# Rows of the recurrence asked for five blocks ahead in every block, and scatters one by one behind GpSimd's diagonals

## The chip, the cores and the metric

The kernel runs on one core of a Trainium2 chip. Five engines work beside each other, each with its own instruction stream in order: TensorE (PE; its weight loads are listed as PEld), VectorE (DVE), ScalarE (ACT), GpSimd (POOL) and SyncE (SP), which issues nearly all plain DMAs. GpSimd issues the indirect DMAs, the scatters. The metric is the device time of one execution in microseconds.

## The reference

Two stages. A recurrence (batch 4, 8 heads, 768 steps, head size 48) gives rows of 8 x 48 = 384 numbers, one per token; a mixture of 8 experts sends each of the 3072 rows through the one expert with the largest logit.

```
state = 0                                   # per batch and head, 48 x 48
for t in range(768):
    cur    = (u * k_t) outer v_t
    y_t    = r_t @ (state + cur)
    state  = w_t[:, None] * state + k_t outer v_t      # w between 0.8 and 0.95

x = y as (3072, 384)
e   = argmax(x @ w_gate);  g = softmax(x @ w_gate)[e]
out = g * (relu(x @ w1[e]) @ w2[e])         # w1[e]: 384 x 1024, w2[e]: 1024 x 384
```

## The kernel before, in words

**Blocks.** The 768 steps are cut into 6 chunks of 128, times 4 batches: 24 blocks, chunk by chunk (block n is chunk n // 4, batch n % 4). Within a block the recurrence is products of 128 x 128 matrices: k times suffix products of w (`kh`) against r times prefix products of w (`rh`) gives the part inside the chunk (`ap`), which is merged through a causal mask into `at`, whose diagonal carries u; `at` times v plus the state's part (`yp`, from `gbd`) gives y.

**Order.** All engines run in the order in which `iteration(n)` writes the instructions; nothing is reordered. Iteration n, from -3 to 23, is a software pipeline: it prepares block n + 3 on VectorE (suffix scan, line 409; product, 421; prefix scan, 427; product, 369) and GpSimd (product rk, 362), turns block n + 1 (diagonals of `at` on ScalarE, 403, and GpSimd, 391) and finishes block n on TensorE and VectorE (`pe_a`, 531; merge by `copy_predicated`, 434; `pe_av`, 566). GpSimd's product of line 362 is held back until VectorE has finished the reciprocal behind the suffix scan (413), and its diagonal (391) until VectorE has finished the prefix scan of block n + 3 (427); both are marked as dependencies.

**Rows of blocks.** `load(n)` brings w, r and k of block n, 580.5 KB, into a ring of 6 buffers (line 111); `load_v(n)` brings v, 192 KB, into one of 5 (line 120). All plain DMAs go through SP's queue in order. The ring's buffer for block n + 6 is free once block n has been prepared, that is in iteration n - 3. Heads that don't fit the 128 partitions take a way through DRAM: `hop_out(n)` (two DMAs, 374) writes parts of `kh` and `rh`, and `hop_in(n)` (380) reads them back as `xk`; SP waits in front of the read for the landing of the write. `pe_a(n)` uses `xk` for its last heads; in block 0, 8 warming products (`pe_warm`, line 526) stand in front of those.

**When rows are asked for.** Blocks 0 and 1 come in parts before the loop, and the w part of block 2. Iterations -3 to 0 ask for block n + 5 (in -3 that is block 2, whole, and the k and r parts of block 2 are asked for again at the end of that iteration). Iteration 0 asks for blocks 6 and 7 as well, and from 1 on it is block n + 7:

```
        if n > 0:
            load(n + 7)
        ...
            load_v(n + 4)
        hop_in(n + 2)
        if n <= 0:
            load(n + 5)
        ...
        hop_out(n + 3)
```

**Routing.** When y of a whole chunk is there, logits, argmax and a running count give each token a row number in its expert's list in DRAM (`xs`). `scatter(c, bs)` (line 730) sends the 128 rows of each batch in `bs` there by an indirect DMA, followed by a small memset on GpSimd (736). `prefill(e)` (352) writes default rows into the part of an expert's list that may stay empty. Chunks 0 and 1 are scattered in iterations 10 to 15, chunks 2 and 3 in 18 to 21, chunk 4 in 23; most stand between GpSimd's product (362) and its diagonal (391).

**Experts.** The first expert's weights come in 12 parts from iteration `W0` on (`load_part`), and six of them are split into a high and a low half from `H0` on (ScalarE makes the high half, line 263). Behind iteration 21, `Part(0, 96)` reads the first 192 rows of expert 0's list (line 283), waiting for all scatters up to there; their transposes (317) stand at the end of iteration 22. Then the last chunk's rows are routed, the experts are sorted by count, and experts run one by one (lines 327, 339, 1019).

Of the kernel before, what the change touches and what calls it, by code (L numbers as in the profile page):

```python
# [17 lines left out]
B, H, S, D = 4, 8, 768, 48  # L18
E, DM, FF = 8, 384, 1024
# [27 lines left out]
PD = 2  # L47
XC = DM + 2
OOB = 1 << 20
W0, H0 = 9, 14  # L50
WMIN, WMAX = 0.7, 1.05


# [5 lines left out]
def rwkv_moe_kernel(ctx, tc, rkw, vv, ub, wgp, wg, w1, w2, wc, out):  # L59
# [36 lines left out]
    def xtile(shape, name):  # L96
        pool, tag = xbanks[nth["x"] % len(xbanks)]
        nth["x"] += 1
        return pool.tile(shape, F32, name=name, tag=tag)
# [3 lines left out]
    def load(n, parts=((0, RW),)):  # L103
        if n >= NB:
            return
        if n == 0:
            for i in range(LD):
                ring.append(ld.tile([P, 4 * XC], F32, name="rkwt", tag="rkwt"))
        t = ring[n % LD][:, 0:RW]
        for lo, hi in parts:  # L110
            nc.sync.dma_start(t[:, lo:hi], rkw[n][:, lo:hi])
        blk[n] = dict(
            w=t[:, 0:NW], r=t[:, NW:NW + NR].rearrange("p (q c) -> p q c", c=C),
            k=t[:, NW + NR:].rearrange("p (q c) -> p q c", c=KW))

    def load_v(n):
        if n >= NB:
            return
        v = ld.tile([P, DM], F32, name="vt", tag="vt", bufs=5)
        nc.sync.dma_start(v, vv[n])  # L120
        blk[n]["v"] = v
# [14 lines left out]
    def keep_warm(t, n):  # L136

        for i in range(n):
            nc.tensor.matmul(t, ones, wz[:, 0:t.shape[1]], start=True, stop=True)
# [210 lines left out]
    def prefill(e):  # L350
        rows = (CMAX - LEAST) // 4
        nc.sync.dma_start(xs[e, LEAST:CMAX, :].rearrange("(p j) c -> p j c", j=4), zrow[:rows].unsqueeze(1).broadcast_to([rows, 4, XC]))

    def real(n):
        return 0 <= n < NB
# [21 lines left out]
    def hop_in(n):  # L377
        if real(n) and "kr" in blk.get(n, ()):
            blk[n]["xk"] = t = xk[n % 3]
            nc.sync.dma_start(t, hop[n % 3])  # L380

    def head_rows(n, q, j):
        d = blk[n]
        rs = slice(64 * j, 64 * j + D)
        if q < NQ:
            return d["kh"][rs, q, 1:KW], d["rh"][rs, q, :]
        return d["xk"][rs, 1:KW], d["xk"][rs, KW:]
# [114 lines left out]
    def pe_warm(k):  # L502
        if k:
            keep_warm(xtile([P, BANK], "wrm")[:, 0:384], k)
# [15 lines left out]
    def pe_a(n):  # L520
        if real(n):
            d = blk[n]
            d["ap"] = psT.tile([P, 2, BANK], F32, name="ap", tag="t").rearrange("p j (q c) -> p j q c", c=C)
            for q in range(NP_):
                if n == 0 and q == NQ:
                    pe_warm(8)
                for j in range(2):
                    kh, rh = head_rows(n, q, j)
                    for i in range(2):
                        hs = slice(64 * i, 64 * i + 64)  # L530
                        nc.tensor.matmul(d["ap"][hs, j, q, :], kh[:, hs], rh, start=True, stop=True)  # L531
# [195 lines left out]
    def scatter(c, bs=range(B)):  # L727
        xr = ch["xr", c]
        for b in bs:
            i = nc.gpsimd.indirect_dma_start(out=xsf, out_offset=bass.IndirectOffsetOnAxis(ap=ch["pi", c, b], axis=0),  # L730
                                             in_=xr[:, b, :], in_offset=None, bounds_check=E * NTOK - 1, oob_is_err=False)
            for k in scat:
                tc.declare_no_dep(i.ins, k, reason="rows of different tokens")
            scat.append(i.ins)

            nc.gpsimd.memset(none, 0.0)
# [37 lines left out]
    def late_splits(half, ks):  # L774
        for k in ks:
            t, i, n, p = late[k]
            split_piece(t, stg[0, i], i, n, p, half)

    def iteration(n):
# [8 lines left out]
        lot = (ROUTED, 0, B)  # L788
        pair = (NCH - 1, 0, 2)
        if n > 0:  # L790
            load(n + 7)
        if 1 <= n <= E:
            prefill(n - 1)
        if W0 <= n < W0 + 12:
            i, p = divmod(n - W0, 3)
            if p == 0:
                stg[0, i] = wst.tile([P, 1536], F32, name="wst", tag="wst")
            load_part(stg[0, i], one, i, p)
        if n > 0:
            load_v(n + 4)  # L800
        hop_in(n + 2)
        if n <= 0:
            load(n + 5)
        if n == 0:
            load_v(2)
# [2 lines left out]
        act_g(n, (NQ,))  # L808
        act_y(n - 1)
        pe_a(n)  # L810
        if n == 0:
            dve_at(n)
# [16 lines left out]
            weigh(whole)  # L829
        if n == NB - 2:  # L830
            late_splits("h", range(0, 3))
        if n in (10, 11):
            scatter(0, (2 * n - 20, 2 * n - 19))
        if 12 <= n < 16:
            scatter(1, (n - 12,))
        if 18 <= n < 22:
            scatter(2 + (n - 18) // 2, (n % 2 * 2, n % 2 * 2 + 1)[0:1 if n == 18 else 2])
        if n == NB - 1:
            scatter(ROUTED)
        if whole and b == 1:  # L840
# [51 lines left out]
            load(2, PARTS[1:])  # L892
        if -3 < n < 0:
            load_v(n + 2)
        if n == 0:
            for i in (6, 7):
                load(i)
                load_v(i - 3)
        if n >= 0:
            pool_diag(n + 1)  # L900
        if n == 18:
            scatter(2, (1,))
        if n == NB - 1:
            scatter(c, (0, 1))
        if whole and b == 0:
# [429 lines left out]
```

## Time and profile before

| | us |
|---|---|
| median of 3 runs | 415.96 |
| the runs | 417.9, 415.96, 411.45 |
| the profiled execution's own time | 417.89 |
| its span, first to last instruction | 416.2 |
| TensorE busy | 389.2 (94%) |
| VectorE busy | 259.5 (62%) |
| ScalarE busy | 222.6 (53%) |
| GpSimd busy | 112.9 (27%) |

The mean granted clock of TensorE is 0.948 of its full speed of 2.4 GHz. The DMA engines moved 72.38 MB. Busy shares are means over stages: up to about 160 us the blocks run, with VectorE near full, and behind it the experts, with TensorE at 94% or more. So a stage is read from its own stretch: from the waits in it and from the order of the instructions, with their start and duration.

### The profile page before, as it was taken

To read this page: it belongs to the slowest core of one execution; us is meant where nothing else is said; L and a number is where in the kernel's file an instruction comes from. 1 tells how busy PE (TensorE), PEld (TensorE's weight loads), DVE (VectorE), ACT (ScalarE), POOL (GpSimd) and SP (SyncE) were. 2 spreads that over 40 slices of the span, in tenths; PEclk is the share of its full clock that TensorE was granted. 3 is DMA by queue.
4 is the path that set the end of the run, shared out by engine and by line. 5 is a ranking of instruction groups with operands and counts; after the bars stand their busy time and mean duration, and the time that the engine had idled before them with its cause. 6 is when DMAs were issued, how large, how long until landed. Compare 5 with 4: busy or idle time off the path is not lost.

```text
span 416.2 us, 10076 instructions
## 1 busy us (share of the span) xinstructions
PE 389.2 (94%) x3810; PEld 356.1 (86%) x3810; DVE 259.5 (62%) x522; ACT 222.6 (53%) x597; POOL 112.9 (27%) x174
## 2 busy tenths in 40 slices
PE   8775999989898979999898999999999999999994
PEld 6564988878787758989887899999999999999994
DVE  7585789998799453447758475374483582842321
ACT  3454698969797841316737374383473573630210
POOL 4152122674359343100110032032051060021002
PEclk9988699999999995599999999999999999999998
DMA  6589879899957421295959825825727617011001
GB/s 184 159 250 341 257 212 252 245 325 286 308 132 215 120 78 58 62 324 168 238 163 285 283 83 131 292 83 164 263 94 222 246 41 226 2 53 37 17 4 53
DMA packets 40785, 72.38 MB, mean 174 GB/s; under 512 B 6319, under 2 KB 28570, under 8 KB 40732
## 3 DMA queue, kind: packets, MB, share of 16 engines
q1 hardware_dynamic: 36124, 62.21, 48.7%
q0 software_dynamic: 4608, 9.48, 6.9%
q8 instruction: 31, 0.51, 0.5%
q14 instruction: 22, 0.18, 0.1%
HBM read 57.40 MB, written 14.61 MB: 173 GB/s over the span
## 4 chain that ended last, share of the span: by engine, by line
PE 63%; DVE 11%; DMA 11%; ACT 7%; issue 5%; SPq 2%; POOL 0%; another core or an unknown queue 0%; POOLq 0%; ACTq 0%; DVEq 0%
PE bank L327 24%; PE bank L1019 17%; PE opt L339 8%; DMA rkwt<-in_rkw_dram 4%; ACT at L403 2%; DVE suf L409 2%; DVE pre L427 2%; PE yq L573 2%; PE yp L566 2%; PE yp L544 2%; PE pt L317 2%; DMA xk<-hop 2%; PE ap L531 2%; PE op L1008 2%; DMA wct<-in_wc_dram 1%
## 5 line engine op out<-in xcount | busy, mean ns | idle before, releaser
L289 POOL DMA_INDIRECT out_dram<-ot,xg x26 | 35.9, 1382 | 164.7 <-DVE ot L1009 101.3
L327 PE MATMUL bank<-xl,w1h 128*128 128x384 f32 (+5 forms) x168 | 59.0, 352 | 0.0
L327 PE MATMUL bank<-xh,w1l 128*128 128x384 f32 (+5 forms) x168 | 58.7, 350 | 0.0
L265 DVE TENSOR_TENSOR w2l<-wst,w2h 128x512 fp32r<-128x512 f32 x48 | 30.8, 686 | 41.4 <-ACT w2h L263 41.2
L327 PE MATMUL bank<-xh,w1h 128*128 128x384 f32 (+5 forms) x168 | 52.7, 351 | 1.6 <-DVE hl L330 1.6
L403 ACT ACTIVATE at<-ident,ct 128x128 f32<-128x128 f32 x144 | 46.8, 392 | 0.1
L434 DVE COPY_PREDICATED at<-cmask,ap 128x1024 f32<-128x1024 int32 x24 | 31.4, 1309 | 20.8 <-PE ap L531 12.0
L730 POOL DMA_INDIRECT xs<-xr,pi x24 | 27.4, 1142 | 25.0 <-DVE xr L641 10.0
L327 PEld LDWEIGHTS bank<-xh,w1h 128*128 128x128 f32 x168 | 31.3, 188 | 2.8 <-DVE hl L330 2.0
L1019 PE MATMUL bank<-hhl,w2h 128*128 128x432 f32 (+4 forms) x120 | 33.5, 356 | 0.0
L362 POOL TENSOR_TENSOR rk<-rkwt 128x384 f32<-128x384 f32 x24 | 22.1, 919 | 40.0 <-DVE pre L413 29.3
L1024 ACT ACTIVATE oT<-bank 128x464 f32<-128x464 f32 (+4 forms) x15 | 7.8, 523 | 46.1 <-PE bank L1019 46.1
L265 DVE TENSOR_TENSOR w1l<-wst,w1h 128x512 fp32r<-128x512 f32 x48 | 31.2, 686 | 2.0 <-ACT w1h L263 2.0
L329 ACT ACTIVATE hhl<-bank 128x384 fp32r<-128x384 f32 (+7 forms) x35 | 16.4, 480 | 29.9 <-PE bank L327 20.9
L327 PEld LDWEIGHTS bank<-xh,w1l 128*128 128x128 f32 x168 | 31.6, 188 | 0.8
L327 PEld LDWEIGHTS bank<-xl,w1h 128*128 128x128 f32 x168 | 31.6, 188 | 0.7
L330 DVE SCALAR_TENSOR_TENSOR hl<-bank,hh 128x384 fp32r<-128x384 f32 (+7 forms) x37 | 19.3, 532 | 19.5 <-ACT hh L329 19.2
L263 ACT ACTIVATE w1h<-wst 128x512 fp32r<-128x512 f32 x48 | 28.8, 628 | 3.2 <-DMA wst<-in_w_dram 2.3
L566 PE MATMUL yp<-at,vt 128*48 128x128 f32 x384 | 29.6, 293 | 0.4 <-issue 0.4
L329 ACT ACTIVATE hh<-bank 128x384 fp32r<-128x384 f32 (+7 forms) x37 | 17.1, 473 | 21.5 <-PE bank L327 19.4
L263 ACT ACTIVATE w2h<-wst 128x512 fp32r<-128x512 f32 x48 | 27.4, 622 | 2.0 <-DMA wst<-in_w_dram 0.9
L330 DVE SCALAR_TENSOR_TENSOR hhl<-bank,hhl 128x384 fp32r<-128x384 f32 (+7 forms) x35 | 18.6, 541 | 13.7 <-ACT hhl L329 11.8
(172 smaller groups left out, 934.7 us busy)
## 6 DMA issues: line engine op xcount, KB each, us to landing
rkwt<-in_rkw_dram SPq DMA_DIRECT2D x22, 580.5 KB
wst<-in_w_dram SPq DMA_DIRECT2D x48, 256.0 KB
wst<-in_w_dram SPq DMA_DIRECT2D x14, 768.0 KB
vt<-in_vv_dram SPq DMA_DIRECT2D x24, 192.0 KB
wct<-in_wc_dram SPq DMA_DIRECT2D x24, 192.0 KB
xg<-xs SPq DMA_DIRECT2D x6, 579.0 KB
xk<-hop SPq DMA_DIRECT2D x24, 112.4 KB
xs<-zrow SPq DMA_DIRECT2D x8, 289.5 KB
```

Source lines behind the costliest of these rows:

```text
L263: nc.scalar.activation(hi, st[:, cs], AF.Copy)
L265: nc.vector.tensor_tensor(out=lo, in0=st[:, cs], in1=hi.bitcast(F32), op=ALU.subtract)
L289: i = nc.gpsimd.indirect_dma_start(out=out[:, :], out_offset=bass.IndirectOffsetOnAxis(ap=t.bitcast(I32)[:, q, DM + 1:DM + 2], axis=0), in ...
L327: nc.tensor.matmul(hp, a, x[:, j, :], start=(i == 0), stop=(i == 8))
L329: nc.scalar.activation(hh, hp, AF.Relu)
L330: nc.vector.scalar_tensor_tensor(out=hl, in0=hp, scalar=0.0, in1=hh.bitcast(F32), op0=ALU.max, op1=ALU.subtract)
L339: nc.tensor.matmul(op, hs[f][x == "l"][:, cs], w2v(wt, "h" if part == "hl" else "l", f), start=(i == 0), stop=(i == 23))
L403: nc.scalar.activation(blk[n]["at"][:, j, q], ident, AF.Copy, scale=blk[n]["ct"][:, head(q, j):head(q, j) + 1])
L434: nc.vector.copy_predicated(out=d["at"].rearrange("p j q c -> p (j q) c"), mask=cmask.unsqueeze(1).broadcast_to([P, 2 * NP_, C]), data=d[" ...
L566: nc.tensor.matmul(d["yp"][o:o + D, q % 2, q // 2, :], d["v"][:, h * D:(h + 1) * D], d["at"][:, j, q, :], start=(n < B and q < 2), stop=(q ...
L730: i = nc.gpsimd.indirect_dma_start(out=xsf, out_offset=bass.IndirectOffsetOnAxis(ap=ch["pi", c, b], axis=0), in_=xr[:, b, :], in_offset=No ...
L1019: nc.tensor.matmul(pp, w, a, start=(i == 0), stop=(i == 23))
```

## The change

The rows of block n + 5 are asked for in every iteration from -2 on; iteration -3 no longer asks for the whole block 2, and iteration 0 asks for nothing beyond block 5. v comes two blocks ahead in every iteration. The prefills start in iteration 2 instead of 1, the first expert's weight parts in 10 instead of 9, and their splits in 15 instead of 14. In block 0 three warming products stand in front of the last heads, not eight. The scatters of chunks 0 and 1 stand one per iteration in iterations 10 to 17, behind GpSimd's diagonal (`pool_diag`); of chunks 2 and 3 those of iterations 18 to 21 stand one behind the diagonal, and one or two at the old place from 19 on.

```diff
-W0, H0 = 9, 14
+W0, H0 = 10, 15
@@ pe_a
                 if n == 0 and q == NQ:
-                    pe_warm(8)
+                    pe_warm(3)
@@ iteration
         if n > 0:
-            load(n + 7)
-        if 1 <= n <= E:
-            prefill(n - 1)
+            load(n + 5)
+        if 2 <= n < 2 + E:
+            prefill(n - 2)
         if W0 <= n < W0 + 12:
...
         if n > 0:
-            load_v(n + 4)
+            load_v(n + 2)
         hop_in(n + 2)
-        if n <= 0:
+        if -3 < n <= 0:
             load(n + 5)
         if n == 0:
             load_v(2)
...
-        if n in (10, 11):
-            scatter(0, (2 * n - 20, 2 * n - 19))
-        if 12 <= n < 16:
-            scatter(1, (n - 12,))
-        if 18 <= n < 22:
-            scatter(2 + (n - 18) // 2, (n % 2 * 2, n % 2 * 2 + 1)[0:1 if n == 18 else 2])
+        for i in {19: (1,), 20: (3,), 21: (5, 6)}.get(n, ()):
+            scatter(2 + i // B, (i % B,))
         if n == NB - 1:
             scatter(ROUTED)
...
-        if n == 0:
-            for i in (6, 7):
-                load(i)
-                load_v(i - 3)
         if n >= 0:
             pool_diag(n + 1)
-        if n == 18:
-            scatter(2, (1,))
+        if 10 <= n < 18:
+            scatter((n - 10) // B, ((n - 10) % B,))
+        for i in {18: (0,), 19: (2,), 20: (4,), 21: (7,)}.get(n, ()):
+            scatter(2 + i // B, (i % B,))
```

## Rows read from the trace of the kernel before

**Rows 1.** Page, clock granted to TensorE in 40 equal slices, in tenths.
```profile
PEclk9988699999999995599999999999999999999998
```

**Rows 2.** Chain that ended last, in time order: start us, length us, what.
```profile
7.60 3.97 DMA rkwt<-in_rkw_dram
...
32.38 7.15 DMA xk<-hop
...
83.14 5.98 DMA rkwt<-in_rkw_dram
```

**Rows 3.** VectorE's merges: start, length, line, operation [idle before, what ended it].
```profile
30.97 1.30 DVE L434 COPY_PREDICATED at<-cmask,ap 128x1024 f32<-128x1024 int32 x1
...
40.44 1.30 DVE L434 COPY_PREDICATED at<-cmask,ap 128x1024 f32<-128x1024 int32 x1 [4.81 <-PE ap L531]
...
53.54 1.32 DVE L434 COPY_PREDICATED at<-cmask,ap 128x1024 f32<-128x1024 int32 x1 [1.12 <-PE ap L531]
...
67.42 1.32 DVE L434 COPY_PREDICATED at<-cmask,ap 128x1024 f32<-128x1024 int32 x1
```

**Rows 4.** SP's DMA issues up to 30 us: start, length, line, what.
```profile
14.30 0.42 SPq L111 DMA_DIRECT2D rkwt<-in_rkw_dram  x1
...
21.28 0.84 SPq L374 DMA_DIRECT2D hop<-kr  x2
...
25.10 0.32 SPq L380 DMA_DIRECT2D xk<-hop  x1
...
29.66 1.09 SPq L111 DMA_DIRECT2D rkwt<-in_rkw_dram  x1
```

**Rows 5.** VectorE up to 20 us: block 0's product, then blocks 2, 0, 3.
```profile
5.99 0.55 DVE L369 TENSOR_TENSOR kr<-rkwt,pre 128x384 f32<-128x384 f32 x1
...
14.82 0.56 DVE L421 TENSOR_TENSOR kr<-rkwt,suf 128x387 f32<-128x387 f32 x1 [2.04 <-DMA rkwt<-in_rkw_dram]
...
17.25 1.29 DVE L434 COPY_PREDICATED at<-cmask,ap 128x1024 f32<-128x1024 int32 x1
19.52 0.97 DVE L409 TENSOR_TENSOR_SCAN suf<-rkwt,sufone 128x390 f32<-128x390 f32 x1 [0.98 <-DMA rkwt<-in_rkw_dram]
```

**Rows 6.** Stretches: length, then each engine's busy us, clock, DMA share, GB/s.
```profile
36.00:38.00 2.00, 0.00 (x0) 0.00 (x0) 0.00 (x0) 0.30 (x2) 0.38 (x1) 1.00 1.06 364
...
40.00:50.00 10.00, 10.00 (x122) 9.06 (x118) 6.87 (x11) 5.99 (x18) 1.31 (x2) 0.58 0.90 252
```

**Rows 7.** Page, costliest groups: line, operation, count, busy us, mean ns.
```profile
L263 ACT ACTIVATE w1h<-wst 128x512 fp32r<-128x512 f32 x48 | 28.8, 628 | 3.2 <-DMA wst<-in_w_dram 2.3
```

**Rows 8.** VectorE at three places between 82 and 129 us.
```profile
82.31 0.96 DVE L409 TENSOR_TENSOR_SCAN suf<-rkwt,sufone 128x390 f32<-128x390 f32 x1
...
84.54 1.31 DVE L434 COPY_PREDICATED at<-cmask,ap 128x1024 f32<-128x1024 int32 x1 [0.81 <-POOL at L391]
...
127.81 1.13 DVE L421 TENSOR_TENSOR kr<-rkwt,suf 128x387 f32<-128x387 f32 x1
```

**Rows 9.** GpSimd in order of time, two scatters and a product.
```profile
80.53 2.13 POOL L730 DMA_INDIRECT xs<-xr,pi  x1 [0.84 <-DMA hop<-kr]
...
82.97 1.08 POOL L730 DMA_INDIRECT xs<-xr,pi  x1 [0.21 <-issue]
...
104.06 0.91 POOL L362 TENSOR_TENSOR rk<-rkwt 128x384 f32<-128x384 f32 x1 [1.31 <-DVE pre L413]
```

**Rows 10.** SP's hop writes and a read back, 67 to 73 us.
```profile
67.23 0.85 SPq L374 DMA_DIRECT2D hop<-kr  x2
...
72.31 0.34 SPq L380 DMA_DIRECT2D xk<-hop  x1
72.75 0.85 SPq L374 DMA_DIRECT2D hop<-kr  x2
```

**Rows 11.** TensorE's products with the rows read back for block 10.
```profile
77.82 0.40 PE L531 MATMUL ap<-xk 48*64 48x128 f32 x8
```

**Rows 12.** The chain again, first expert's products of 192 columns.
```profile
171.61 5.92 PE bank L327 x27
```

## The prediction

> **What bounds the kernel now.** I read first the slices of the clock, then the chain that ended last, then SP's, VectorE's and GpSimd's instructions in order of time. The clock row shows full speed except around 20 to 50 us and 156 to 177 us [rows 1]. The second half of the span is a TensorE-bound stage that this change does not touch, so what the change can give or take lies in the first 160 us, the 24 recurrence blocks, and it arrives at the end undiluted, because routing, sorting and the experts follow the last block in a chain.
>
> Among the blocks the chain shows three transfers. Block 2's rows are asked for whole, after their first part has landed, and take 3.97 us (from 7.60); a read back from the hop buffer takes 7.15 us (from 32.38); a later load takes 5.98 us (from 83.14) [rows 2]. From block 5 to block 8 the distance from one merge of the causal part (line 434) to the next is (67.42 - 53.54) / 3 = 4.63 us [rows 3]: VectorE then works back to back, and that is the pace if nothing is late.
>
> **The change part by part.** The sum is made against the profiled execution: 417.89 us (span 416.2 plus 1.7 around it), which is 1.93 us above the median 415.96.
>
> *A. Block 2 asked for once.* SP is in order. Before, the whole-block load of 7.60 must land before the k and r parts can be asked for again, and block 3's load goes out at 14.30 only [rows 2, 4]; VectorE stands idle 2.04 us for block 2's k (14.82) and 0.98 us for block 3 (19.52) [rows 5]. After, the two issues of hop 0 can follow block 0's last product, which ends at 5.99 + 0.55 = 6.54 [rows 5]. The read back in front of block 3's load waits for their landing. Nearest row: a hop asked for at 21.28 was read back at 25.10, so 3.82 us [rows 4]. Read back at 10.4, block 3's load at 10.75 instead of 14.30: 3.55 us. Block 3 took 19.52 - 14.30 = 5.2 us to arrive, so it could be scanned at 16.0; VectorE is ready then only if block 0's merge (17.25) moves as well [rows 4, 5]. It does: its last heads wait for the same read back, and with three warming products instead of eight in front of them TensorE is free when it lands. I take 3.5. Ends: 2.0 (the idle 2.04 alone) and 5.0 (the 3.97 of the transfer and the 0.98 of idling). The five warming products cost nothing now, while TensorE waits there; without that wait they would have been in the way, and with fewer the clock could fall, which is kept for rival 4.
>
> *B. No catching up.* At block 0 SP asks for blocks 5, 6 and 7, then for 8 (29.66), with their v, and only then for the hop rows that block 3 needs (32.38) [rows 2, 4]. The DMA engines are full then (1.06, 364 GB/s), and TensorE does nothing from 36 to 38 us [rows 6]. Block 3's merge starts after 4.81 us of idling [rows 3]. Behind it the granted clock is 0.58 on average from 40 to 50 us, mostly the lower level, 1.2 GHz, after that idle stretch [rows 6]. From merge 2 (30.97) to merge 5 (53.54) three blocks take 22.57 us against 3 x 4.63 = 13.89: 8.7 us too long [rows 3]. After, one load and one v a block stand in front of that read back, and the wait should go with the slow clock behind it. The least is the wait itself, 4.8; the most 8.7. I take 7.9, nearer to the second, since the slow clock follows that idle stretch in the rows, and a little less, since the first blocks have extra copies. What is late next is SP's loop, part E.
>
> *C. Prefill, weight parts and their splits one block later.* The same DMAs, one iteration on; they were hidden by VectorE's work and stay so, apart from their share in E. The last of the six splits now meets block 20, where it delays ScalarE's copies for TensorE: one copy of 512 columns is 0.63 us [rows 7]. I take +0.5; ends 0 and +0.6.
>
> *D. Scatters behind the diagonals.* Before, two scatters in front of block 11's diagonal, the first of 2.13 us, keep VectorE's merge waiting 0.81 us (84.54) [rows 8, 9]; this goes. Behind the diagonal GpSimd has an idle stretch before its next product, 1.31 us at 104.06 [rows 9]. A warm scatter takes 1.08 [rows 9], so with its gap it fits, nearly to the full. Queued behind the scatter on GpSimd is that product (line 362); if it is late it meets VectorE's product of line 421, as at 127.81, where that took 1.13 instead of 0.56: 0.57 us [rows 5, 8]. The two cold scatters will do this, and the pairs of blocks 18 to 21 no longer do. Net -0.5; ends -2 and +2. The last scatter before the first rows are fetched goes behind the diagonal of block 22, about one scatter later; SP's load of those rows waits for it, and TensorE's transposes for the load, but these come a whole block after it.
>
> *E. SP's loop.* With the deep lead gone, SP's cycle is: send hop rows, ask for rows, prefill and v, wait for the hop's landing, read it back, send the next. From 67.23 to 72.75 it took 5.52 us, more than VectorE's 4.63 [rows 3, 10]. Before, that lag cost nothing: the read back of 72.31 was used at 77.82 [rows 10, 11]. After, about seven blocks (2 to 8) run without a stall that lets SP catch up: 7 x 0.89 = 6.2 us of lag. The slack of 5.5 us [rows 10, 11], less the landing, plus the lag that was harmless already, covers most of it. I take +1.0; ends 0 and 6.2. The v loads stop waiting for a buffer in SP's queue; what that helps is in this choice.
>
> Sum: -3.5 - 7.9 + 0.5 - 0.5 + 1.0 = -10.4. 417.89 - 10.4 = 407.5; with the profile 1.93 above the median, 405.6. I say **405.5 us**.
>
> **The rivals.**
> *1. The late slow stretch goes too.* From 156 to 177 us the clock is at the lower level [rows 1]; 27 products of the first expert's rows take 5.92 us there, and eight groups of nine run in it [rows 12]. At 2.4 GHz they take at best half, so 72 / 27 x 2.96 = 7.9 us less. Nothing in the change aims at it, but what is in front of it shifts, and where TensorE's gaps fall decides it. With half to all of it: about 399. Chance 0.16.
>
> *2. The wait moves to SP's loop.* If the slack of E is not there, blocks 2 to 8 take 5.52 instead of 4.63: 6.2 us instead of 1.0, so 405.5 + 5.2 = 410.7. For it: the DMA engines are still 0.90 busy from 40 to 50 us, behind the catching up [rows 6], and the bytes per block do not change. Against it: the same loop ran beside blocks of 4.63 us. If the two removals do only the least that A and B allow, the time is about the same: 417.89 - 2.0 - 4.8 + 1.0 - 1.93 = 410.2. Chance of both 0.18.
>
> *3. Scatters beside the scans.* The scatter of 82.97 stood beside VectorE's scan of 82.31 and took 1.08 us, half of the one before it [rows 8, 9]; so I give this little. If it did take longer, the product behind it would be late in each of 14 blocks: 14 x 0.57 = 8.0 us, so 405.5 + 8.0 = 413.5. Chance 0.05.
> The Trainium skill, in "SBUF — State Buffer", section "SBUF: two separate sides", speaks against this change: VectorE and GpSimd share a port pair, held by one of them for a whole instruction, and a DMA issued by GpSimd cannot have its descriptors written while VectorE holds it. By that rule a scatter moved beside the scan, which reads two SBUF tiles, could wait for the scan's end, and the sum would be that of rival 3. The row of 82.97 does not agree with it for this scan.
>
> *4. Slower: rows come too late.* The lead shrinks from four blocks to two, 2 x 4.63 = 9.3 us between asking and scanning. It decides from the point where a load takes longer than that; the one of 83.14 took 5.98 [rows 2]. If loads pass 9.3 us in blocks 8 to 18, where SP's lag has built up and the weights come in beside one scatter a block, VectorE waits in each, TensorE idles and its clock falls as behind block 3, where two blocks took (53.54 - 40.44) / 2 = 6.55 us [rows 3]. That is 11 x (6.55 - 4.63) = 21.1 us: 405.5 + 21.1 = 426.6, slower than before. Fewer warming products would push the same way. Chance 0.07.
>
> **How the numbers follow.** The forecast has 0.54; its own range is 401 to 410, with A, B and E at their ends, not all at once. Rivals 1 to 4 have 0.16, 0.18, 0.05 and 0.07. About 2% (8.3 us; below 407.6, above 424.3) is what a measurement can tell from no change. Three quarters of the forecast's chance lie below 407.6, 0.41; with rival 1, faster has 0.57. The rest of the forecast with 2 and 3 is within 2%, 0.36; rival 4 is slower, 0.07. The range that leaves out no more than 2 in 10 goes from 397 (rival 1, most of it) to 414 (rival 3).
>
> **What would show it.** A: block 3's load asked for near 10.7, its scan near 16, no wait for block 2's k. B: no stretch of 2 us without TensorE work around 26 to 32 us, merge 5 near 53.54 - 11.4 = 42, no low clock in front of it. D: no merge released by GpSimd's diagonal; line 421 not longer than 0.6 except behind cold scatters. E: distances of merges 5 to 8 near 4.7; at 5.5, rival 2. VectorE waiting at line 409 for rows in blocks 8 to 18 would make the prediction wrong, and so would a low clock that comes at another place.

## Result: about 5.6 us faster, half of what the steps added up to

Over 20 runs of each kernel on one chip the changed kernel takes 410.33 us in the median, the kernel before 416.13; the ratio is 0.9865, 95% interval 0.9833 to 0.9897. That is 5.6 us less (1.35%), inside the forecast's range but not the 10.4 us of its sum; it is below the 2% that count as a clear difference. Some executions run at a lower granted clock and some per cent longer, and the ratios leave these out, so a ratio can differ from that of the medians. In a later comparison on a chip where the kernel before takes 401.55 us the changed kernel takes 394.97: ratio 0.9828 (0.9779 to 0.9876). The profiled execution of the changed kernel (417.78 us, span 416.1) had a long stretch of low clock behind 134 us, so only its first 127 us are compared with before.

The page of the changed kernel, granted clock in 40 slices of 10.4 us:

```profile
PEclk9985699999999555599999999999999999999998
```

Against [rows 1] the slow stretch of the blocks is still there, in slices 3 to 5 (the late one too). VectorE's merges show what became of the 11.4 us by which merge 5 should have moved. The changed kernel, VectorE in order of time (start, length, line, operation, idle before it and what ended that):

```profile
13.68 1.29 DVE L434 COPY_PREDICATED at<-cmask,ap 128x1024 f32<-128x1024 int32 x1
14.87 0.95 DVE L409 TENSOR_TENSOR_SCAN suf<-rkwt,sufone 128x390 f32<-128x390 f32 x1
...
27.45 1.29 DVE L434 COPY_PREDICATED at<-cmask,ap 128x1024 f32<-128x1024 int32 x1
...
33.66 1.31 DVE L434 COPY_PREDICATED at<-cmask,ap 128x1024 f32<-128x1024 int32 x1 [1.54 <-ACT gbd L464]
...
40.95 1.30 DVE L434 COPY_PREDICATED at<-cmask,ap 128x1024 f32<-128x1024 int32 x1 [2.62 <-ACT gbd L464]
...
49.94 1.32 DVE L434 COPY_PREDICATED at<-cmask,ap 128x1024 f32<-128x1024 int32 x1 [2.34 <-PE ap L531]
...
54.55 1.31 DVE L434 COPY_PREDICATED at<-cmask,ap 128x1024 f32<-128x1024 int32 x1
```

Merge 0 (13.68; 17.25 in [rows 5]) is 3.57 us earlier and merge 2 (27.45; 30.97 in [rows 3]) 3.52. Merge 5 (49.94; 53.54) is 3.60 earlier: from merge 2 to merge 5 the changed kernel needs 22.49 us, the kernel before 22.57. The idle 4.81 in front of block 3's merge is gone (merge 3 comes 6.78 us earlier), and by merge 5 nothing is left of that. From merge 5 to merge 8 the step is 4.60 us, as before.

The early gain is in SP's queue. The changed kernel, SP's issues:

```profile
6.59 0.78 SPq L374 DMA_DIRECT2D hop<-kr  x2
7.42 0.90 SPq L111 DMA_DIRECT2D rkwt<-in_rkw_dram  x2
9.39 0.34 SPq L380 DMA_DIRECT2D xk<-hop  x1
9.78 0.43 SPq L111 DMA_DIRECT2D rkwt<-in_rkw_dram  x1
```

Block 3's rows are asked for at 9.78 instead of 14.30 [rows 4], and its scan at 14.87 waits for nothing.

What took the place of the wait is seen on TensorE. The changed kernel, the two products behind idle time between 20 and 29 us:

```profile
21.73 0.81 PE L510 MATMUL cp<-ubt,rk 128*128 128x8 f32 x6 [1.81 <-DVE sst L444]
...
27.68 1.17 PE L510 MATMUL cp<-ubt,rk 128*128 128x8 f32 x6 [1.32 <-DVE sst L444]
```

and its stretches (length, busy us of PE, PEld, DVE, ACT, POOL, then clock, DMA share, GB/s):

```profile
20.00:30.00 10.00, 6.56 (x104) 5.92 (x106) 9.66 (x14) 5.51 (x18) 4.28 (x21) 0.90 0.71 219
30.00:40.00 10.00, 10.00 (x116) 8.93 (x116) 6.66 (x14) 6.77 (x20) 2.62 (x4) 0.50 0.90 251
40.00:50.00 10.00, 10.00 (x157) 8.92 (x149) 4.99 (x9) 5.53 (x20) 1.43 (x3) 0.58 0.84 226
```

The clock falls to 1.2 GHz at about 28 us, behind two gaps of TensorE (1.81 and 1.32 us), and stays there to about 48. The busy share of 100% hides it: TensorE is never idle from 30 to 50 us because each product takes longer (six products of line 510 take 1.17 us at 27.68, 0.81 at 21.73), and VectorE now waits for it. In the kernel before [rows 6] a low clock followed the wait for block 3's hop rows. But it had fallen there once already, ahead of that wait and behind a gap at the same line. The kernel before, TensorE, and the stretch from 28 to 30 us:

```profile
26.05 0.81 PE L510 MATMUL cp<-ubt,rk 128*128 128x8 f32 x6 [1.93 <-DVE sst L444]
...
28.00:30.00 2.00, 2.00 (x35) 1.64 (x35) 1.97 (x4) 1.90 (x6) 1.40 (x7) 0.50 1.03 362
```

### The profile page after: what moved, and what is told of

Same layout as the page of the kernel before. It is cut to its first block, busy times and chain, and to the rows that moved or that the text cites. A ratio compares the mean times of both kernels' runs of the same rounds, so it can differ in the third digit from the quotient of the medians.

```text
span 416.1 us, 10055 instructions
## 1 busy us (share of the span) xinstructions
PE 394.1 (95%) x3805; PEld 362.6 (87%) x3805; DVE 260.3 (63%) x522; ACT 223.1 (54%) x597; POOL 113.1 (27%) x174
## 3 DMA queue, kind: packets, MB, share of 16 engines
HBM read 56.81 MB, written 14.61 MB: 172 GB/s over the span
## 4 chain that ended last, share of the span: by engine, by line
PE 75%; DMA 7%; DVE 7%; ACT 4%; issue 4%; SPq 1%; POOL 0%; POOLq 0%; DVEq 0%; ACTq 0%
PE bank L327 23%; PE bank L1013 17%; PE opt L339 7%; PE yp L566 5%; PE ap L531 5%; DMA wst<-in_w_dram 3%; PE yp L544 3%; PE yq L573 3%; PE cp L510 3%; DMA hop<-kr 3%; PE lp L580 2%; PE pt L317 2%; PE dp L557 2%; DMA rkwt<-in_rkw_dram 2%; PE op L1002 2%
## 5 line engine op out<-in xcount | busy, mean ns | idle before, releaser
L566 PE MATMUL yp<-at,vt 128*48 128x128 f32 x384 | 32.3, 311 | 1.6 <-DVE at L434 1.6
L566 PEld LDWEIGHTS yp<-at,vt 128*48 128x48 f32 x384 | 25.4, 141 | 2.7 <-DVE at L434 1.9
```

The costliest lines, as they stand in the source:

```text
L566: nc.tensor.matmul(d["yp"][o:o + D, q % 2, q // 2, :], d["v"][:, h * D:(h + 1) * D], d["at"][:, j, q, :], start=(n < B and q < 2), stop=(q ...
```

## Experiments

Each kernel was timed beside the kernel before on its chip; that took 401.24 us in the first four, 401.55 in the next four, 415.65 in the next three and 402.23 in the last, so the ratios are compared and not the times. The table gives the start of merges 2, 5, 12, 16 and 20 in the one profiled execution of each kernel, so small differences between rows mean little. "Fillers" are the small products of experiment 2.

| kernel | 2 | 5 | 2 to 5 | 12 | 16 | 20 | ratio (interval) |
|---|---|---|---|---|---|---|---|
| before | 30.97 | 53.54 | 22.57 | 89.14 | 109.73 | 132.28 | 1 |
| after | 27.45 | 49.94 | 22.49 | 85.22 | 104.69 | 126.58 | 0.9865 (0.9833 to 0.9897) |
| after, other chip | 26.95 | 47.81 | 20.86 | 82.50 | 102.84 | 124.10 | 0.9828 (0.9779 to 0.9876) |
| block 2 once, alone | 27.15 | 49.12 | 21.97 | 84.73 | 105.44 | 127.37 | 0.9913 (0.9876 to 0.9951) |
| catching up restored | 27.63 | 48.00 | 20.37 | 82.99 | 101.88 | 123.56 | 0.9868 (0.9814 to 0.9922) |
| old scatters | 26.82 | 47.93 | 21.11 | 83.24 | 104.39 | 126.32 | 0.9830 (0.9783 to 0.9876) |
| early fillers | 27.57 | 47.59 | 20.02 | 82.30 | 101.18 | 122.76 | 0.9842 (0.9789 to 0.9895) |
| fillers, read back first | 25.95 | 46.51 | 20.56 | 97.34 | 128.79 | 158.59 | 1.1081 (1.102 to 1.1142) |
| fillers, fillers at block 4 | 26.83 | 47.73 | 20.90 | 82.45 | 107.71 | 128.55 | 0.9845 (0.9785 to 0.9906) |
| fillers, prefill from block 6 | 26.61 | 41.14 | 14.53 | 81.70 | 102.05 | 124.03 | 0.9891 (0.9809 to 0.9974) |
| fillers, prefill from block 3 | 26.87 | 41.55 | 14.68 | 76.53 | 102.14 | 123.32 | none |
| prefill from block 3, no fillers | 28.18 | 45.94 | 17.76 | 80.92 | 101.00 | 123.64 | 0.9893 (0.9841 to 0.9946) |
| fillers, one prefill in the gap | 27.58 | 42.19 | 14.61 | 80.27 | 99.57 | 121.27 | 0.9846 (0.9778 to 0.9914) |
| nine weight parts left out | 27.32 | 42.26 | 14.94 | 77.92 | 98.10 | 119.48 | 0.9796 (0.9742 to 0.9849) |

**1. One part alone, or one part undone.** The kernel before with block 2 asked for once:

```diff
-        if n <= 0:
+        if -3 < n <= 0:
             load(n + 5)
```

> The kernel before with part A alone: block 2 is asked for once; deep lead, eight warming products and scatters as before. Theory 1: A alone moves every merge up to block 2 by 2 to 3.5 us and is worth 2 to 3.5 us in all, about 413. Rival (the long hop wait of block 3 takes it back, since the burst of loads is there still): within 1 us of before, 415 to 416.

Measured: 397.27 us, ratio 0.9913 (0.9876 to 0.9951), that is 3.5 us of 401.24. The long wait of block 3 is still there, 4.96 us. This kernel, TensorE:

```profile
35.65 0.70 PE L531 MATMUL ap<-xk 48*64 48x128 f32 x8 [4.96 <-DMA xk<-hop]
```

Part A is worth what the forecast gave it, even with the eight warming products still in place. Next, the changed kernel with the deep lead put back:

```diff
-            load(n + 5)
+            load(n + 7)
...
-            load_v(n + 2)
+            load_v(n + 4)
...
+        if n == 0:
+            for i in (6, 7):
+                load(i)
+                load_v(i - 3)
```

> The changed kernel with the deep lead and the catching up put back (blocks 6 and 7 in iteration 0, then n + 7; v four blocks ahead): only part B is undone. Theory 1: the hop wait of block 3 is back, 4 to 5 us, but the clock is low from 28 to 48 us in the changed kernel as well, so the time is within 2 us of the changed kernel, 409 to 412. Rival (B gave what was forecast and something else took it): 6 to 8 us slower than the changed kernel, 416 to 418.

Measured: 397.05 us, ratio 0.9868 (0.9814 to 0.9922), merge 5 at 48.00. It catches up at block 0 again, and its read back of block 3's hop rows takes 6.88 us, from 27.49; the clock is at 0.50 from 22 to 42 us. Yet it is no slower from merge 2 to merge 5 than the changed kernel (20.37 against 20.86), and the ratios differ by 0.4%, or 1.6 us, with intervals that overlap. The edit undoes part B and with it E, the lag of SP's loop. So B and E together are worth 1.6 us at the most likely, and from the two intervals at most about 4.5, not the 6.9 that the sum gave them (-7.9 and +1.0).

The changed kernel with the scatters where they stood before:

> The changed kernel with all scatters at their places before the change: only part D is undone. Theory 1: D is worth 0 to 2 us, so 410 to 412, and the scatters of iterations 10 to 16 go back from about 1.5 us to 1.03 us each, with GpSimd's product (line 362) again idle before it. Rival (the scatters of block 21 in front of the diagonal bring the clock down at 134 us and cost more than the others gain): 2 to 5 us faster than the changed kernel.

Measured: 395.67 us, ratio 0.9830 (0.9783 to 0.9876); the changed kernel itself has 0.9828. Part D moves the time by nothing that can be seen. In this kernel, as in the next ones, a wait for hop rows is back, at block 4. Old scatters, TensorE:

```profile
36.34 0.45 PE L531 MATMUL ap<-xk 48*64 48x128 f32 x8 [1.31 <-DMA xk<-hop]
```

**2. Holding the clock up.** 28 small products on spare columns behind the transposes of blocks 2 and 3, so that the gaps near 22 and 27 us are partly filled:

```diff
...
+            keep_warm(kb[:, NQ * P:], {2: 16, 3: 12}.get(n, 0))
```

> The changed kernel with 16 and 12 small filler products on TensorE (128 columns, into unused columns of the kp tile) behind the transposes of blocks 2 and 3, where its profile shows TensorE idle for 1.8 and 1.3 us before the clock falls to 1.2 GHz at 28 us. Theory 1 (the gain of part B was lost to the clock: TensorE runs blocks 2 to 5 at 1.2 GHz, 7.5 us a block instead of 4.7 to 5): the clock stays at full speed from 20 to 50 us, merges 2 to 5 come in about 15 us instead of 22.5, and the time falls by 6 to 8 us against the changed kernel, to about 403. Rival (blocks 2 to 5 are paced by the DMA engines and SP's loop): the clock may stay up, but merges 2 to 5 still take over 20 us, and the time stays within 1.5 us of 410.

Measured: 396.18 us, ratio 0.9842 (0.9789 to 0.9895), no different from the changed kernel. The clock held, at 1.00 up to 38 us, and merge 3 came 4.59 us behind merge 2. Then TensorE waited for block 4's hop rows (merge 4 5.81 us later), the clock fell behind 38 us, and merge 5 came 9.62 us after that. SP's queue of this kernel shows the place:

```profile
28.77 1.04 SPq L374 DMA_DIRECT2D hop<-kr  x2
29.91 1.67 SPq L111 DMA_DIRECT2D rkwt<-in_rkw_dram  x1
31.62 0.73 SPq L352 DMA_DIRECT2D xs<-zrow  x1
32.40 0.59 SPq L120 DMA_DIRECT2D vt<-in_vv_dram  x1
33.16 1.49 SPq L380 DMA_DIRECT2D xk<-hop  x1
```

and its TensorE the price:

```profile
37.35 0.45 PE L533 MATMUL ap<-xk 48*64 48x128 f32 x8 [1.87 <-DMA xk<-hop]
```

The read back of block 4 stands behind a row load, the first prefill (line 352) and a v load. The clock alone was not what was missing.

**3. Which part of SP's queue.** The changed kernel itself went along for comparison:

> The changed kernel itself, beside variants of it and the kernel before on the same chip. Expected: 5 to 6 us below the kernel before; the clock falls to its lower level near 28 us, merge 5 (block 5's first causal merge) near 49.9 us. If undoing single parts (catching up, scatters) cost nothing, this stands within 2 us of the two kernels that undid them, at 0.983 to 0.987 of before.

Measured: 394.97 us, ratio 0.9828 (0.9779 to 0.9876). On this chip, too, block 4's hop rows are late, and merge 5 is 11.15 us behind merge 4. The changed kernel on this chip, TensorE:

```profile
36.05 0.45 PE L531 MATMUL ap<-xk 48*64 48x128 f32 x8 [0.92 <-DMA xk<-hop]
```

The clock falls behind the gap near 22 us here too (1.58 us), but only from about 23 to 27 us, and again behind this wait, from about 37 to 47 us. So the low stretch from 28 to 48 us of the first chip is not in every execution, while the time from merge 2 to merge 5 is nearly as long (20.86 us against 22.49).

With the fillers, and the read back in front of the loads of its block:

```diff
         if n > 0:
+            hop_in(n + 2)
             load(n + 5)
...
-        hop_in(n + 2)
+        if n <= 0:
+            hop_in(n + 2)
```

> The changed kernel with the early fillers (28 small products behind the transposes of blocks 2 and 3) and, in SP's queue, the read back of the hop rows put in front of the row load, the prefill and the v load of its block. Theory 'the wait moved into SP's queue' (block 4's hop rows read back at 33.2 us, behind a load, a prefill and a v load, landed at 37.3): read back issued near 31.2, landed by 33.5, no wait for them at 35.5, clock stays full past 38 us, merge 5 near 41 to 42 us in place of 47.6, total 5 to 6 us below the one with fillers alone. Rival 'the clock falls anyway, at the next gap of TensorE': merge 5 at 46 to 48 us, total as with fillers alone. Rival 'the loads come late instead': VectorE waits for rows of block 6 or 7, and half of the gain is lost.

Measured: 444.82 us, ratio 1.1081 (1.102 to 1.1142): far slower, and the third case came true from block 6 on: 18 scans of line 409 wait for rows, for 0.25 to 4.59 us. SP waits for the landing of the hop rows before it may read them back, and now the row load stands behind that wait. Read back first, SP:

```profile
28.29 0.87 SPq L374 DMA_DIRECT2D hop<-kr  x2
33.90 0.31 SPq L380 DMA_DIRECT2D xk<-hop  x1
34.25 0.43 SPq L111 DMA_DIRECT2D rkwt<-in_rkw_dram  x1
```

and VectorE, which waits for rows:

```profile
52.50 0.97 DVE L409 TENSOR_TENSOR_SCAN suf<-rkwt,sufone 128x390 f32<-128x390 f32 x1 [2.65 <-DMA rkwt<-in_rkw_dram]
```

The blocks come 7.5 us apart (from merge 5 to merge 20), and the mean DMA share from 20 to 130 us drops to 0.60. It is rival 4's mechanism: the lead of two blocks does not last when the load is queued behind that wait.

With the fillers, and the prefills two a block from block 6 on:

```diff
-        if 2 <= n < 2 + E:
-            prefill(n - 2)
+        if 6 <= n < 6 + E // 2:
+            prefill(2 * n - 12)
+            prefill(2 * n - 11)
```

> The changed kernel with the same early fillers, and the eight prefills of the expert rows two a block from block 6 on, not one a block from block 2 on. Theory 'the bytes of load, prefill and v in front of block 4's read back make it late': without the prefill the read back is issued about 0.7 us earlier and lands up to 1.5 us earlier, near 35.8 to 36.5 us; TensorE's wait of 1.87 us shrinks to under 1 us, merge 5 at 42 to 47 us depending on whether the clock holds. Rival 'order of the queue, not bytes': the wait stays above 1.3 us and the total stays within 1 us of fillers alone; blocks 6 to 9 may get a wait of their own.

Measured: 403.08 us in the median (394.93 to 413.84), ratio 0.9891 (0.9809 to 0.9974). The expected part happened and more: without the prefill in block 2 TensorE has no idle time over 0.6 us from 26 to 52 us, the clock stays up, and merge 5 comes at 41.14. Late prefill, SP, block 4's read back:

```profile
28.52 0.47 SPq L111 DMA_DIRECT2D rkwt<-in_rkw_dram  x1
29.04 1.63 SPq L120 DMA_DIRECT2D vt<-in_vv_dram  x1
31.41 0.34 SPq L380 DMA_DIRECT2D xk<-hop  x1
```

It is 1.75 us earlier than with the fillers alone. But with two prefills a block the steps from merge 8 to 11 are 6.85, 7.07 and 8.15 us, in place of 6.26, 4.99 and 4.79, and by merge 12 the lead over the changed kernel on this chip is down from 6.67 us to 0.80 (81.70 against 82.50).

With the fillers, and twelve more products of 384 columns in front of the hop heads of blocks 4 and 5:

> The changed kernel with the early fillers, and eight and four more products of 384 columns in front of the hop heads of blocks 4 and 5, where TensorE waits for the read back (1.3 and 0.6 us of filler at 2.4 GHz). Theory 'the low clock, not the wait itself, is what costs 6 us between merge 4 and merge 5': the wait of block 4 stays (merge 4 near 38 us), the clock stays at the upper level from 38 to 45 us, merge 5 near 43 us in place of 47.6, total 4 to 5 us below fillers alone. Rival 'the wait behind SP's queue goes on in block 5': merge 5 at 46 or later with a full clock.

Measured: 397.0 us, ratio 0.9845 (0.9785 to 0.9906). It is not a clean test: the wait had moved to block 3. Fillers at block 4, TensorE:

```profile
32.16 0.45 PE L533 MATMUL ap<-xk 48*64 48x128 f32 x8 [1.92 <-DMA xk<-hop]
```

The clock fell there, before the new fillers came, and merge 5 is where it was.

**4. Prefills spread so that no block has two early.** With the fillers:

```diff
-        if 2 <= n < 2 + E:
-            prefill(n - 2)
+        if 3 <= n < 10:
+            prefill(n - 3)
+        if n == 9:
+            prefill(7)
```

> The changed kernel with the early fillers, and the prefills one a block in blocks 3 to 8 and two in block 9, so that none stands in block 2 and none is doubled before the last. Theory 'bytes of block 2's prefill make the hop rows late, and two prefills a block cost 2 us a block later': merge 5 near 41 to 42 us as with all prefills from block 6 on, blocks 5 to 8 at 4.6 us, one longer block (by 2 us) near block 9, merge 12 near 77 to 78 us in place of 82.5 of the changed kernel; total 4 to 5 us below the changed kernel, ratio to before 0.970 to 0.975. Rival 'the lag only moves one block on': a wait for the hop rows of block 5, merge 5 at 45 us or later, and the total within 1.5 us of the changed kernel.

Measured: 411.54 us in the median of six (404.37 to 414.76) beside 415.65 of before; the times spread too widely for a ratio. The trace tells more than the time. Prefill from block 3, VectorE's merges 5, 15 and 16:

```profile
41.55 1.32 DVE L434 COPY_PREDICATED at<-cmask,ap 128x1024 f32<-128x1024 int32 x1 [0.61 <-PE ap L533]
...
94.00 1.30 DVE L434 COPY_PREDICATED at<-cmask,ap 128x1024 f32<-128x1024 int32 x1 [1.34 <-PE ap L533]
102.14 1.32 DVE L434 COPY_PREDICATED at<-cmask,ap 128x1024 f32<-128x1024 int32 x1 [2.84 <-PE ap L533]
```

Blocks 2 to 5 take 14.68 us, close to the 13.89 that the prediction hoped for, and merge 12 is 8.7 us ahead of the changed kernel's on the first chip (6.0 on the other). By merge 16 the lead is 2.6 (0.7). The longer block that was expected for the two prefills of block 9 did not come: from merge 8 to merge 12 it takes 21.10 us, as on the other chip the changed kernel (20.90). Its TensorE says what ate it:

```profile
93.38 0.45 PE L533 MATMUL ap<-xk 48*64 48x128 f32 x8 [1.19 <-DMA xk<-hop]
```

The wait for hop rows, and the clock behind it (0.50 from 96 to 100 us), have come back eleven blocks later, at block 15.

The same prefills without fillers:

> The changed kernel with those prefills alone, without fillers. Theory 'the prefill's bytes are the cause, the clock follows the wait': no wait for hop rows of block 4, clock low at most for a few us after 22, merge 5 near 42 to 43, total within 1.5 us of the one with fillers. Rival 'the gaps of TensorE at 20 to 22 and 26 to 28 us lower the clock by themselves, without any wait': clock low for over 8 us between 22 and 45, merge 5 at 46 or later, total within 1.5 us of the changed kernel.

Measured: 410.37 us, ratio 0.9893 (0.9841 to 0.9946). This time block 4's hop rows are not late, and the clock falls all the same. No fillers, TensorE:

```profile
22.10 1.28 PE L510 MATMUL cp<-ubt,rk 128*128 128x8 f32 x6 [1.92 <-DVE sst L444]
```

and its stretches:

```profile
20.00:22.00 2.00, 0.17 (x2) 0.00 (x0) 1.44 (x4) 0.75 (x2) 0.16 (x1) 1.00 0.34 122
22.00:34.00 12.00, 11.90 (x127) 10.84 (x131) 9.57 (x16) 6.39 (x18) 5.43 (x23) 0.51 0.84 252
```

The rival holds for the clock, and nearly for merge 5 (45.94): the clock falls behind the gap of 1.92 us with no such wait, and up to merge 5 the kernel needs 17.76 - 14.68 = 3.1 us more than with fillers. The length of the gap alone does not decide it: with the early fillers alone a gap of 1.79 us in front of the same line was not followed by a fall. But merge 16 (101.00) is earlier than with the fillers (102.14). With the eighth prefill asked for in block 1, near 19 us, and the rows that it writes made ready two iterations earlier:

> The changed kernel with the early fillers, prefills one a block in blocks 3 to 9, and the eighth one asked for behind block 1's v (near 18.6 us), where the DMA share is 0.2 to 0.4 from 20 to 22 us. If its 0.3 MB fit into that gap: as the one with two in block 9, without the longer block there, 1 to 2 us less, ratio to before 0.966 to 0.972. If it makes block 5's row load or block 3's hop rows late: merge 3 and all behind it 1 to 3 us later, and nothing is gained over two in block 9.

Measured: 409.67 us, ratio 0.9846 (0.9778 to 0.9914). Merge 20 at 121.27 is the earliest among the kernels that do the whole work, and no hop rows are late by more than 0.52 us; the ratio is not better than the changed kernel's.

**5. Fewer bytes.** However early merge 12 was in the changed kernel and its variants (76.5 to 85.2, the read back first left aside), merge 20 came between 121 and 129. The last run takes nine of the twelve weight parts out of blocks 10 to 21, so its first expert computes with wrong weights:

```diff
-            if p == 0:
-                stg[0, i] = wst.tile([P, 1536], F32, name="wst", tag="wst")
-            load_part(stg[0, i], one, i, p)
+            if n == W0:
+                stg[0, 0] = wst.tile([P, 1536], F32, name="wst", tag="wst")
+            stg[0, i] = stg[0, 0]
+            if i == 0:
+                load_part(stg[0, i], one, i, p)
```

> The kernel with fillers and the prefill from block 3 on, with 3 of the 12 weight parts loaded in blocks 10 to 21 (the other nine, 2.3 MB, are left out; their splits read the first piece again, so the first expert's weights are not the reference's). Theory 'the transfers set the pace': in every kernel so far the mean DMA share from 20 to 130 us is 0.86 or 0.87 (253 to 258 GB/s), and merge 20 ends near 123 to 127 us however early merge 12 is (76.5 to 85.2). 2.3 MB less at 258 GB/s are 9 us; VectorE's own pace there is about 4.75, so from merge 12 to merge 20 38 to 41 us in place of 46.8; merge 20 at 114.5 to 118, and a total 6 to 9 us below that kernel's undisturbed 404.4 (or the same ratio on another chip: 0.955 to 0.965 of before). Rival 'the round trip of the hop rows (write, wait, read back), whatever the bytes': the distance of read backs stays at 5.3 us or more, merge 20 at 121 or later, total within 2 us. Rival 'scatters and GpSimd set it': merges 13 to 18 stay 5.2 to 6 us apart, released by GpSimd's product.

Measured: merge 20 at 119.48. From merge 12 to merge 20 it takes 41.56 us, where the same kernel with all its bytes takes 46.79; read backs come 5.0 us apart (40.07 us for eight), and the clock never falls. Both sizes are a little outside what the theory said (38 to 41 us, 114.5 to 118).

It looks like a proof that transfers set the pace, but it is none. The same eight blocks take 40.46 us with the early fillers, 40.57 with the catching up restored, 41.00 with one prefill in the gap and 41.36 in the changed kernel, all with every byte. So 2.3 MB less made nothing shorter than it is elsewhere; what is gone is the wait of the kernel compared with, at block 15, and its low clock. Whether the missing bytes removed it, or chance, these runs do not show: one prefill in the gap, with all bytes, does not have it either.

What these kernels share is the work of VectorE and TensorE. Merge 8 to merge 20, in this order: before, changed, early fillers, nine weight parts left out (length, busy us of PE, PEld, DVE, ACT, POOL, then clock, DMA share, GB/s):

```profile
67.42:132.28 64.86, 60.86 (x1237) 51.72 (x1232) 58.79 (x115) 54.05 (x179) 36.33 (x60) 1.00 0.85 255
63.75:126.58 62.83, 60.04 (x1245) 51.64 (x1237) 58.62 (x115) 54.04 (x180) 35.11 (x58) 1.00 0.91 273
61.39:122.76 61.37, 59.51 (x1229) 51.09 (x1221) 58.70 (x115) 53.36 (x177) 34.47 (x56) 1.00 0.91 278
56.41:119.48 63.07, 59.78 (x1233) 51.29 (x1233) 58.49 (x113) 54.03 (x178) 34.18 (x56) 1.00 0.86 251
```

VectorE is busy 58.5 to 58.8 us in all of them, 4.9 us a block, and idle for the rest: 6.1, 4.2, 2.7 and 4.6 us. TensorE is busy even longer, 59.5 to 60.9 us; which of the two sets the pace is not shown. As long as VectorE's work in these twelve blocks stays as it is, no order of the transfers can give back more than that.

The total, 394.72 us and ratio 0.9796 (0.9742 to 0.9849), is far from the 0.955 to 0.965 expected. The profiled execution took 390.48 us against 395.48 of the changed kernel's on a chip of about the same time before, so it kept the 4.6 us of merge 20; the other five took 392 to 396, at a mean granted clock of 0.982 to 0.991 against its 0.996. No trace of them shows where it was low.

None of the kernels that compute everything beats the changed one by more than the intervals of the two.

## Why the prediction was right in range, and which step failed

That 410.33 lies between 397 and 414 is owed to A and to the width of the range, not to the sum: it is just outside the forecast's own 401 to 410, and more than half of the chance (0.57) stood on a gain of 2%, which did not come.

**A held.** 3.5 was forecast; merges 0 and 2 moved by 3.57 and 3.52, and the part alone gave 3.5 us (2.0 to 5.0 by its interval). Block 3's rows were asked for at 9.78 (forecast 10.75) and scanned at 14.87 (16.0), both a little earlier, because the read back came 2.8 us behind the hop rows' issue and not 3.82 [rows 4].

**B failed: -7.9 was forecast, -1.6 measured by the ratios (for B and E together), about nothing between merges 2 and 5.** The wait of [rows 3] went as said. What failed is "the wait should go with the slow clock behind it"; the prediction's own sign against itself, a low clock at another place, came. Even the least that the step allowed, 4.8, is not in the time. A stall of TensorE lay ready in two other places. One is a gap of TensorE near 22 us, and a smaller one near 27 (1.81 and 1.32 us in the changed kernel, both in front of line 510). The run without fillers shows that the clock falls behind the first with no hop rows of block 4 late. The trace of the kernel before has the like of it, 1.93 us in front of 26.05, with the clock at 0.50 from 28 us, ahead of the wait that the step held responsible. Both gaps of the changed kernel stand behind rows that VectorE waits for: the scan of 20.16 after 1.34 us of idling, and the scan of 26.04, which the chain that ended last puts behind block 5's load, asked for at 21.19. The changed kernel, VectorE, and that piece of the chain:

```profile
20.16 0.97 DVE L409 TENSOR_TENSOR_SCAN suf<-rkwt,sufone 128x390 f32<-128x390 f32 x1 [1.34 <-DMA rkwt<-in_rkw_dram]
...
24.62 1.33 DVE L493 COPY kg<-kt 128x96 f32<-128x96 f32 x1
26.04 1.04 DVE L409 TENSOR_TENSOR_SCAN suf<-rkwt,sufone 128x390 f32<-128x390 f32 x1
...
21.19 4.82 DMA rkwt<-in_rkw_dram
```

The second place is block 4's read back, behind a load, a prefill and a v load. The runs separate the two. From merge 2 to merge 5 it takes 20.9 to 22.5 us with both in place, 20.0 with fillers against the first alone, 17.8 with no prefill in front of block 4's read back and no fillers, and 14.5 to 14.9 with both taken away. So 4.63 a block was about the right floor; the step's error was to take the floor for what would come.

**Behind block 5 there was little left to win.** With both places mended and the prefills from block 6, merge 5 is 6.7 us ahead of the changed kernel's on the same chip (41.14 against 47.81), but the time is not better by more than the intervals. Part of the lead goes in waits that come later: two prefills a block (merges 8 to 11), hop rows of block 15 with a low clock behind them, or shorter waits between merges 5 and 12. What ends each of these waits is seen; what makes the rows late at just that block is open. And no later block makes it good, since from merge 8 on VectorE's own work is 4.9 us a block, not the 4.63 that [rows 3] show for blocks 5 to 8: the kernel before is idle there for 6.1 us in all, the changed one for 4.2. The mean DMA share from 20 to 130 us, 0.84 to 0.88 in every kernel but the one with the read back first, does not show that the transfers are the bound: about the same bytes move in about the same time, whatever the kernel waits for. A keeps its gain because it starts SP's loop earlier (first read back at 9.39 instead of 13.91) and all blocks behind it; it also takes one load, 0.59 MB, out.

**C and E** cannot be told apart from the rest: no run undoes C alone, and E was undone only together with B. E's sign of success came (merges 5 to 8 4.60 apart, no lag of 6.2 us), but SP's queue did bite, in the main at block 4, where E spread a lag over blocks 2 to 8. **Rival 2** came nearest, in part by luck: its numbers, 410.7 and 410.2, are almost that measured, but blocks 5 to 8 did not slow down, and its second form counts 4.8 for B. No run shows the price of Part C's late split.

**D**, -0.5, came to nothing: 0.9830 without it against 0.9828 with it. Merge 11 is no longer released by GpSimd's diagonal, as said. But merge 13 now stands behind the memset that follows a scatter, for 0.60 us, and a scatter behind a diagonal takes 1.53 us, not 1.08 [rows 9]. The changed kernel, GpSimd:

```profile
98.91 1.53 POOL L730 DMA_INDIRECT xs<-xr,pi  x1 [0.34 <-issue]
100.44 0.09 POOL L736 MEMSET none<- 1x1 f32 x1
100.50 0.92 POOL L362 TENSOR_TENSOR rk<-rkwt 128x384 f32<-128x384 f32 x1
```

and VectorE, merge 13 and the time of that scatter:

```profile
90.62 1.32 DVE L434 COPY_PREDICATED at<-cmask,ap 128x1024 f32<-128x1024 int32 x1 [0.60 <-POOL none L736]
...
98.63 0.96 DVE L409 TENSOR_TENSOR_SCAN suf<-rkwt,sufone 128x390 f32<-128x390 f32 x1
99.96 1.31 DVE L434 COPY_PREDICATED at<-cmask,ap 128x1024 f32<-128x1024 int32 x1
101.17 0.67 DVE L421 TENSOR_TENSOR kr<-rkwt,suf 128x387 f32<-128x387 f32 x1
```

The scatter ends 0.85 us after the scan does, here and in the blocks with the scans of 83.88, 88.60 and 93.89 (0.84 to 0.85); at the old place, beside no scan, it takes 1.03. So rival 3's mechanism exists: the rule of the Trainium skill, "SBUF — State Buffer", section "SBUF: two separate sides", that the two engines share a port pair held for a whole instruction, agrees with these rows (0.85 us behind the scan's end), and the prediction was wrong to hold the row of 82.97 against it. That scatter overlapped the scan of 82.31 for 0.30 us only, and it too ended behind it, by 0.78. The price is small: the scatter is 0.45 us longer than the 1.08 that the sum used, VectorE's product of line 421 meets the product behind it and takes 0.66 to 0.68 us in four of five blocks, above the 0.6 that the prediction set as a sign, and not the 1.13 of rival 3, and blocks 15 and 16 take 4.74 and 4.73 where blocks 6 to 8, without scatters, take 4.60.

**Rival 1** did not come, and its stretch goes with the chip in these traces, not with the change: on the chip of the other comparison the changed kernel's clock is full from 48 us to the end, and on the first it is low from 134 to 178. The three kernels traced on the chip where the kernel before takes 415.65 us have such a stretch too; on the three chips where it takes 401 to 402 only the kernel with the read back first does.

## What to carry to other kernels

Before a stall is credited with the low clock behind it, look in the same trace for an earlier fall, and for the gap of TensorE in front of it: here one of 1.93 us stood ahead of the wait. Test by filling the gap and removing the next wait together, and each alone. To know what a stage can still give, add up the busy time of its busiest engines over the same blocks in each variant (here VectorE, 58.5 to 58.8 us of 61 to 65, and TensorE, 59.5 to 60.9); a mean DMA share that stays the same is no proof that the transfers are the bound. When bytes are left out, compare with every kernel that has them all, and not with one that happened to wait. In an in-order queue, do not put a load behind a wait for something else: here it made the kernel 43 us slower than the kernel before.

## What the hardware showed

A gap of 1.92 us of TensorE near 22 us was followed by 12 us at a granted clock of 0.51, in which the records show TensorE 99% busy; with 16 small products in front of the same place (1.06 us) and the same prefills the gap was 1.21 and the clock stayed at 1.00; with the early fillers alone it stayed there behind a gap of 1.79. So a busy share near 100% is no sign that an engine is at its pace.

A scatter of GpSimd took 1.53 us where VectorE's scan ran beside it and 1.03 elsewhere, and ended 0.85 us behind the scan. VectorE's copy of line 493 took 1.33 us at 24.62, not 0.20 as at 53.09, beside GpSimd's memsets:

```profile
24.70 1.05 POOL L204 MEMSET gbd<- 112x256 f32 x4
```

It was as long in the kernel before (1.33 at 28.95). It does not hold the scan behind it: there the scan starts 0.67 us after the copy's start. Moving those memsets was not tried.

Two prefills of 290 KB in each of blocks 6 to 9, beside about 1 MB of rows, v and hop rows a block, went with steps 0.6 to 3.4 us longer from merge 8 to merge 11; one in each of blocks 6 to 8 of the changed kernel did not, nor did two in block 9 alone.
